# The second batch's keys turned by VectorE instead of TensorE, and entries of two hand-written orders moved, in an attention, feed-forward and routed-experts kernel

## The chip, the cores and the metric

One NeuronCore of a Trainium2 chip runs the whole kernel in one launch. The metric is device microseconds of one execution; several are made, and the median counts. TensorE multiplies and transposes into PSUM, VectorE (DVE), ScalarE (ACT) and GpSimd (POOL) do the element work, and SyncE (SP) issues most DMAs.

## The reference

```python
# attention: 4 batches, 8 heads of 64; 512 local and 32 global positions
k_all, v_all = concat([k_g, k_l]), concat([v_g, v_l])
out_g = softmax(scale * q_g @ k_all.T) @ v_all          # global queries see all keys
s_ll  = where(|i - j| <= 32, scale * q_l @ k_l.T, -1e9)  # local queries: a window ...
s_lg  = scale * q_l @ k_g.T                              # ... and the globals
out_l = softmax(concat([s_lg, s_ll])) @ concat([v_g, v_l])
x = concat([out_g, out_l]) as 2176 tokens x 512
# feed-forward with squared relu
x = (maximum(x @ w_in, 0) ** 2) @ w_out                  # 512 -> 2048 -> 512
# routed experts
do_compute = x @ w_skip > 0
e = argmax(x @ w_gate);  p = softmax(x @ w_gate)[e]      # 8 experts, each 512 -> 1024 -> 512
out = x;  out[do_compute] += p * (maximum(x @ w1[e], 0) @ w2[e])
```

## The kernel before, in words

The local tokens are cut into 8 blocks `j` of 256 (two tiles of 128 tokens, `a` and `b`), two blocks to a batch. Block `j` needs attention (`attention_block(j)`), then the feed-forward (`ffn_block(j)`), then routing (`route`, once for each tile), which fills a table of slots for the experts. The experts come last.

All engines run their instructions in the order in which the program emits them, and this order is written out by hand. `SEQ` is the list for blocks 0 to 2 and the feed-forwards of blocks 0 and 1; afterwards `EVEN` and `ODD` alternate: while `ffn_block(j)` runs, they emit attention of block `j+1` and the routing of block `j-1`. One pass of the loop with even `j` uses `EVEN`: that is `j` = 2, 4, 6. A word of a list emits one step:

- `F0`, `E0`, `I0`, `H0` (and 1; in `EVEN` and `ODD` plain `F`, `E`): one unit of a feed-forward. Units alternate between a first product (`first`, lines 803 to 805, 12 matmuls, then relu on ACT, line 807) and a second product (`second`, lines 828 to 830, 6 matmuls) that is emitted behind the squaring of the newer hidden block and its split into a high part `gh` (ACT, line 203) and a low part `gl` (line 204). The letter says which engine squares (`F`, `I`: VectorE, line 844; `E`, `H`: ScalarE, line 846) and which makes `gl` (`F`, `E`: GpSimd; `H`, `I`: VectorE).
- `Lk10`, `Lk11`: load the keys of batch 1, heads 0 to 3 and 4 to 7 (`load_k`). `2G`, `20` to `23`: in block 2, which opens batch 1, turn the global keys and the four head pairs of local keys into `kT` (`prep_globals`, `prep_k`). `2q` turns the queries.
- `2a`, `2b`: the next of six steps of a tile's attention. Step 1 emits the scores `sc` of all eight heads (line 484) with mask, maximum and exponentials of half of them (lines 497 to 505); step 2 the other half's; steps 3 and 4 transpose the weights (`ptr`, line 511); step 5 is the product with the values (`po`); step 6 transposes the result.
- `1g`, and `g` in `EVEN`: the next of eight steps of the global queries' attention: scores; transposes `gptr` and their copies `gpT`, `gpTg` (lines 615, 619); value products `gpo` (line 626) with their four scalings into `xg` (line 634); an empty step; and the same four again for the other heads.
- `R00`, `R01` (tiles of block 0), and `r`, `s` in `EVEN`: the next of five steps of `route`: 1 transposes the tile (`x2tr`, line 300) and makes a bf16 copy on ACT (line 713); 2 makes the other two bf16 thirds on VectorE (lines 703 to 705); 3 multiplies with the gates (`pl`, line 725) and finds the expert (VectorE); 4 counts (`pr`, lines 750 and 751) and works out the slot on VectorE (lines 752 to 776; line 766 is the last to read `pr`); 5 puts it in the table (`pt`, line 779).
- `C`, `D`: convert one weight tile (ACT line 271, the low part of the one before on GpSimd or VectorE, line 275). `V`: load value windows. `W`, `A`: fetch and reassemble weights.

PSUM has eight banks, by name of the tile's tag: two `tr` (all transposes, and half of each score tile), one `s`, one `o`, two `h`, two `x2`. In `EVEN`'s passes the tiles `po`, `gpo`, `pl`, `pr` and `pt` all have the tag `o`:

```python
BANKS = {"tr": 2, "s": 1, "o": 1, "h": 2, "x2": 2}
po = ps.tile([P, D], F32, tag=O_TAG, bufs=BANKS[O_TAG], name=f"gpo{b}_{g}")   # O_TAG "o"
pr = ps.tile([P, 2, E], F32, tag=O_TAG, bufs=BANKS[O_TAG], name=f"pr{t}")     # O_TAG "o" for j >= 2
```

Batches 2 and 3 already have their keys turned by VectorE; batches 0 and 1 by TensorE, four transposes of 128x128 for each pair of heads into a `tr` bank (line 376), copied to `kT` by two instructions (lines 378 and 383; on ACT in batch 1). The two ways want the keys loaded in different layouts: for TensorE 4 DMAs of 128 KB for four heads, in pieces of 64 numbers (256 bytes); for VectorE's 32x32 blocks 8 DMAs of 64 KB, in pieces of 32 numbers (128 bytes).

Of the kernel before, what the change touches and what calls it, by code (L numbers as in the profile page):

```python
# [22 lines left out]
    0b A V 0a W 0b V A 1q W W A 0b V 1a W W F0 A W E0 1a W W A W V 1a A F0 W 1a I0 A 1b L9 1a H0 V A A W V E0 W 1a  # L23
    X0 H0 A A E0 H0 W H0 A H0 W 1b E0 Lg1 A A W W A E0 1b W H0 A 1b E0 A H0 A E0 Lv00 A W W W 1g A I0 C 1b A 1g I0 W
    A D H0 Lv01 1g W E0 A E0 A I0 1g W C C 1g C W E0 A 1g Lq2 C Lk10 A H0 1g I0 2q A C C F0 2G Lk11 E0 I0 20 C 1b E0 21
    22 F0 F1 23 C D F0 H1 C C V R00 2a F1 D H1 E1 2a E1 D R00 2a H1 R00 R01 C H1 C C F1 I1 R01 V 2b R01 E1 D A F1
    2a E1 D C H1 2b F1 R00 2a I1 C C H1 D F1 V H1 R00 V F1 R01 C Lq3 E1 D E1 C C R01 F1 2b D C 2b H1 C C 1g F1 H1 2b
    2a E1 F1 D E1 F1 H1 Lv10 V 2b I1 V
"""

EVEN = """
    q E F F r E r a F a E lg F s F r E s E F g a s E a E a F g F r V a F g E r V E lv1 F b g s E F b E E b E V g b F
    b F b F g F s lk1 F g E V g lq F lk0 E
"""

# [17 lines left out]
TURNED = 3  # L53
# [6 lines left out]
def attention_ffn_routed_experts(  # L60
# [22 lines left out]
    nc = tc.nc  # L83
    B, H, SL, D = q_l.shape
# [5 lines left out]
    E, _, F = w1.shape  # L90
# [4 lines left out]
    TPB = SL // P  # L95
# [28 lines left out]
    def stage(name):  # L124
        return wpool.tile([P, 1024], F32, tag="w", name=f"st_{name}{arm[0]}")
# [3 lines left out]
    def pair(name):  # L129
        return ps.tile([P, 4, P], F32, tag="tr", bufs=2, name=name + arm[0])  # L130
# [160 lines left out]
    kT, kin, qT, qin, qgT, vgr = {}, {}, {}, {}, {}, {}  # L291
# [10 lines left out]
    def quadrants(o, src):  # L302
        for r in range(2):
            for half in range(2):
                c = SEG * (2 * r + half)
                for a in range(o.shape[1]):
                    nc.sync.dma_start(o[c:c + SEG, a], src(r)[:, a, :, SEG * half:SEG * (half + 1)])

    def load_k(b, z):
        if b == 0:  # L310
            kin[b, z] = stage(f"k{b}_{z}").rearrange("p (j h d) -> p j h d", h=4, j=TPB)
            t = stage(f"k{b}_{z}_in").rearrange("p (h j d) -> p h j d", h=4, j=TPB)
            nc.sync.dma_start(t, k_l[b, 4 * z:4 * z + 4].rearrange("h (p j) d -> p h j d", j=TPB))
            puts[f"{b}{z}"] = lambda: nc.scalar.copy(kin[b, z], t.rearrange("p h j d -> p j h d"))
            return
        if b < (TURNED + 1) // 2:
            kin[b, z] = stage(f"k{b}_{z}").rearrange("p (j h d) -> p j h d", h=4, j=TPB)
            for h in range(4):
                nc.sync.dma_start(kin[b, z][:, :, h, :], k_l[b, 4 * z + h].rearrange("(p j) d -> p j d", j=TPB))
            return  # L320
        kin[b, z] = stage(f"k{b}_{z}").rearrange("p (a n d) -> p a n d", a=2, d=SEG)
        pairs = k_l[b, 4 * z:4 * z + 4].rearrange("(a r) (n p) d -> r p a n d", r=2, p=SEG)
        quadrants(kin[b, z], lambda r: pairs[r])
# [39 lines left out]
        nc.scalar.copy(qgT[b], tr[:, :, 0:SG])  # L363

    def prep_k(b, p):
        if b >= (TURNED + 1) // 2:
            full = WIN * (KEYS // P)
            src = kin[b, p // 2][:, p % 2].rearrange("p n d -> p (n d)")
            threes = kT[b][:, p, 0:KEYS - SEG].rearrange("p (g c) -> p g c", c=P)[:, :, 0:WIN]
            nc.vector.transpose(out=threes, in_=src[:, 0:full].rearrange("p (g c) -> p g c", c=WIN))  # L370
            nc.vector.transpose(out=kT[b][:, p, KEYS - SEG:KEYS], in_=src[:, full:SL])
            return
        tr = pair(f"ktr{b}_{p}")
        for j in range(TPB):
            two = kin[b, p // 2][:, j, 2 * (p % 2):2 * (p % 2) + 2, :]
            nc.tensor.transpose(tr[:, j, :], two.rearrange("p r d -> p (r d)"), ident)
        q = WIN * (KEYS // P) // TPB
        nc.scalar.copy(
            kT[b][:, p, 0:KEYS - SEG].rearrange("p (g q j) -> p j g q", j=TPB, q=P // TPB)[:, :, :, 0:WIN // TPB],
            tr[:, :, 0:q].rearrange("p j (g q) -> p j g q", q=WIN // TPB),  # L380
        )
        put = nc.vector.tensor_copy if b == 0 else nc.scalar.copy
        put(kT[b][:, p, KEYS - SEG:KEYS].rearrange("p (q j) -> p j q", j=TPB), tr[:, :, q:P])
# [256 lines left out]
    def attention_block(j, S_TAG="s", O_TAG="o", G_TAGS=("s", "o")):  # L640

        b, z = divmod(j, TPB // 2)
        gens = {
            "a": attention(2 * j, S_TAG, O_TAG), "b": attention(2 * j + 1, S_TAG, O_TAG),
            "g": attention_global(b, *G_TAGS),
        }

        def emit(what):
            if what in gens:
                next(gens[what])  # L650
            elif what == "G":
                prep_globals(b)
            elif what == "q":
                prep_q(j)
            elif what in "0123":
                prep_k(b, int(what))
            elif what == "lq":
                if j + 1 < NB:
                    load_q(j + 1)
            elif what in ("lv0", "lv1"):  # L660
                load_v_global(b, int(what[2]))
            elif b + 1 < B:
                load_globals(b + 1) if what == "lg" else load_k(b + 1, int(what[2]))

        return emit
# [649 lines left out]
    with tc.manual_schedule():  # L1315
# [3 lines left out]
        def do(what):  # L1319
# [12 lines left out]
            elif what == "V":  # L1332
                load_v(*divmod(viewed[0], 2))
                viewed[0] += 1
            elif what[0] == "P":
                puts[what[1:]]()
            elif what == "L9":
                nc.sync.dma_start(w9[:, :, 0:E], w_gate.rearrange("(k p) e -> p k e", p=P))
                nc.sync.dma_start(w9[:, :, E:E + 1], w_skip.rearrange("(k p o) -> p k o", p=P, o=1))
            elif what[0] == "L":  # L1340
                load = {"g": load_globals, "k": load_k, "q": load_q, "v": load_v_global}[what[1]]
                load(*map(int, what[2:]))
            elif what[0] in "FEIH":
                square_on[0] = nc.vector if what[0] in "FI" else nc.scalar
                rest_on[0] = nc.gpsimd if what[0] in "FE" else nc.vector
                j = int(what[1])
                if j not in streams:
                    streams[j] = ffn_block(j, 1, (("x2", "x2"), ("s", "o"))[j])
                next(streams[j])
            elif what[0] == "R":  # L1350
                j, z = int(what[1]), int(what[2])
                if (j, z) not in routes:
                    routes[j, z] = route(*outs[j][z], *(("x2",) if j == 0 else ()))
                next(routes[j, z])
            else:
                j = int(what[0])
                if j not in emits:
                    emits[j] = attention_block(
                        j, *(("x2", "x2") if j == 2 else ("s", "o")), (("tr", "tr") if j == 1 else ("s", "o"))
                    )  # L1360
                emits[j](what[1:])
# [75 lines left out]
        for what in TAIL.split():  # L1437
            if what == "T":
                next(ffn, None)
            elif what in "XY":  # L1440
                j = "XY".index(what)
# [39 lines left out]
            elif what[0] in "gp":  # L1481
                e, j = map(int, what[1:])
# [226 lines left out]
```

## Time and profile before

| | |
|---|---|
| median of 3 runs | 692.17 us (690.86 to 692.66) |
| the profiled execution's own time | 692.0 us |
| its span, first to last instruction | 690.3 us |
| TensorE matmul busy | 663.4 us (96%) |
| TensorE weight load busy | 553.0 us (80%) |
| VectorE busy | 423.2 us (61%) |
| ScalarE busy | 344.4 us (50%) |
| GpSimd busy | 180.7 us (26%) |
| mean granted TensorE clock | 0.983 of full speed |

The profile is of one execution. Times in its rows are microseconds from the start of the span. A bracket behind a row is the time that the engine was idle before it, and the instruction that ended the wait.

### The profile page before, as it was taken

Reading aid. Unit: us, or ns where it says so; the run is one execution under the profiler, and the core shown is the slowest. Engines: PE = TensorE matmul, PEld = TensorE weight load, DVE = VectorE, ACT = ScalarE, POOL = GpSimd, SP = SyncE. Lnnn points to the kernel's source line nnn. Section 1 sums busy time; section 2 is a strip of 40 time slices with the busy share of each in tenths; the row PEclk is TensorE's granted clock in tenths of the full one; section 3 lists DMA queues with packets and bytes.
Section 4 is the critical chain, followed back from the end, with each engine's and each line's share of the span. In section 5 each row is a group of like instructions: output and inputs, shape, how many; then the busy total and the mean of one; then the engine's idle time right before and its main releaser. Section 6 shows DMA issues by size and latency. Waiting matters only on the chain. (4 is left out here: it accounts for less than half of the span.)

```text
span 690.3 us, 16621 instructions
## 1 busy us (share of the span) xinstructions
PE 663.4 (96%) x6545; PEld 553.0 (80%) x6545; DVE 423.2 (61%) x1142; ACT 344.4 (50%) x834; POOL 180.7 (26%) x236
## 2 busy tenths in 40 slices
PE   6689999999999999999999999999999999999996
PEld 4466668788888888888888888888987887898875
DVE  1899983874566377367456647535248535816984
ACT  5767567765534444453445453434344324615862
POOL 8000043354222212312222322222212242301321
PEclk8699999999999999999999999999999999999999
DMA  9999844047053441307243402210056588953920
GB/s 274 248 294 249 282 99 109 1 109 149 5 120 65 95 109 36 85 2 149 72 76 90 108 6 85 82 63 32 1 153 192 200 286 300 385 204 111 371 94 21
DMA packets 137503, 93.39 MB, mean 135 GB/s; under 512 B 103541, under 2 KB 110709, under 8 KB 137412
## 3 DMA queue, kind: packets, MB, share of 16 engines
q1 hardware_dynamic: 127104, 70.62, 38.2%
q10 hardware_dynamic: 8292, 15.48, 6.8%
q0 software_dynamic: 2016, 6.09, 2.5%
q8 instruction: 55, 0.90, 0.6%
q14 instruction: 36, 0.29, 0.1%
HBM read 79.91 MB, written 12.66 MB: 134 GB/s over the span
## 5 line engine op out<-in xcount | busy, mean ns | idle before, releaser
L204 POOL TENSOR_TENSOR gl<-g,gh 128x256 fp32r<-128x256 f32 x107 | 79.8, 746 | 238.7 <-ACT gh L203 94.5
L803 PE MATMUL h<-xh,w_in 128*128 128x256 f32 x464 | 134.1, 289 | 0.0
L805 PE MATMUL h<-xh,w_in 128*128 128x256 f32 x464 | 129.8, 280 | 0.2 <-POOL w_in L275 0.2
L804 PE MATMUL h<-xl,w_in 128*128 128x256 f32 x464 | 129.6, 279 | 0.0
L828 PE MATMUL acc<-w_out,gh 128*128 128x512 f32 x232 | 97.0, 418 | 1.2 <-ACT gh L203 1.2
L830 PE MATMUL acc<-w_out,gl 128*128 128x512 f32 x232 | 91.9, 396 | 0.2
L829 PE MATMUL acc<-w_out,gh 128*128 128x512 f32 x232 | 91.5, 395 | 0.0
L803 PEld LDWEIGHTS h<-xh,w_in 128*128 128x128 f32 x464 | 87.1, 188 | 4.5 <-issue 1.0
L804 PEld LDWEIGHTS h<-xl,w_in 128*128 128x128 f32 x464 | 87.2, 188 | 2.7 <-DVE xl L204 0.2
L805 PEld LDWEIGHTS h<-xh,w_in 128*128 128x128 f32 x464 | 87.1, 188 | 0.4 <-POOL w_in L275 0.4
L807 ACT ACTIVATE g<-h 128x256 f32<-128x256 f32 x128 | 48.7, 380 | 66.8 <-PE h L805 45.1
L203 ACT CAST gh<-g 128x256 fp32r<-128x256 f32 x116 | 47.1, 406 | 37.7 <-DVE g L844 35.6
L844 DVE TENSOR_TENSOR g<-h,g 128x256 f32<-128x256 f32 x53 | 22.1, 417 | 69.5 <-ACT g L807 69.4
L505 ACT ACTIVATE sm<-sm,mx 128x128 f32<-128x128 f32 x120 | 41.2, 391 | 43.1 <-DVE mx L502 43.1
L830 PEld LDWEIGHTS acc<-w_out,gl 128*128 128x128 f32 x232 | 43.5, 188 | 12.0 <-POOL gl L204 1.5
L828 PEld LDWEIGHTS acc<-w_out,gh 128*128 128x128 f32 x232 | 43.6, 188 | 8.4 <-ACT gh L203 1.7
L829 PEld LDWEIGHTS acc<-w_out,gh 128*128 128x128 f32 x232 | 43.7, 189 | 5.8
L275 POOL TENSOR_TENSOR w_in<-st_raw_in,w_in 128x512 fp32r<-128x512 f32 x10 | 13.2, 1326 | 74.7 <-ACT w_in L271 74.7
L497 DVE TENSOR_TENSOR sm<-sc,masks_slots 128x512 f32<-128x512 f32 x30 | 20.6, 687 | 14.7 <-PE sc L484 13.5
L846 ACT ACTIVATE g<-g 128x256 f32<-128x256 f32 x63 | 26.2, 415 | 4.1 <-ACT g L807 2.1
L826 PE MATMUL acc<-st_raw_out,gh 128*128 128x512 f32 x48 | 23.9, 618 | 0.8 <-ACT gh L846 0.8
L511 PE MATMUL ptr<-ident,sm 128*128 128x128 f32 x120 | 20.5, 290 | 2.5 <-ACT sm L505 2.4
(649 smaller groups left out, 1446.3 us busy)
## 6 DMA issues: line engine op xcount, KB each, us to landing
st_e<-in_moe_w_dram SPq DMA_DIRECT2D x46, 512.0 KB
st_raw_in<-in_moe_w_in_dram SPq DMA_DIRECT2D x16, 512.0 KB
st_raw_out<-in_moe_w_out_dram SPq DMA_DIRECT2D x16, 512.0 KB
st_e<-in_moe_w_dram ACTq DMA_DIRECT2D x12, 512.0 KB
x2d<-x ACTq DMA_DIRECT2D x19, 256.5 KB
vr<-in_v_l_dram SPq DMA_DIRECT2D x32, 128.0 KB
st_gv<-in_v_l_dram SPq DMA_DIRECT2D x8, 512.0 KB
out_dram<-x ACTq DMA_DIRECT2D x16, 256.0 KB
```

The source lines that it names most:

```text
L203: nc.scalar.copy(hi, src)
L204: (lo_engine or nc.vector).tensor_tensor(out=lo, in0=src, in1=hi.bitcast(F32), op=ALU.subtract)
L505: nc.scalar.activation(sm[:, hh, :], sm[:, hh, :], AF.Exp, bias=mx[:, hh:hh + 1], scale=SCALE, **sums)
L803: nc.tensor.matmul(h, lhsT=wh, rhs=xh[:, k, :], start=(k == 0), stop=False)
L804: nc.tensor.matmul(h, lhsT=wh, rhs=xl[:, k, :], start=False, stop=False)
L805: nc.tensor.matmul(h, lhsT=wl, rhs=xh[:, k, :], start=False, stop=(k == KD - 1))
L807: nc.scalar.activation(g, h, AF.Relu)
L826: nc.tensor.matmul(acc[z], lhsT=gh[:, c], rhs=w, start=first_one, stop=last_one)
L828: nc.tensor.matmul(acc[z], lhsT=gh[:, c], rhs=wh, start=first_one, stop=False)
L829: nc.tensor.matmul(acc[z], lhsT=gh[:, c], rhs=wl, start=False, stop=False)
L830: nc.tensor.matmul(acc[z], lhsT=gl[:, c], rhs=wh, start=False, stop=last_one)
L846: nc.scalar.activation(square, g, AF.Square)
```

## The change

Batch 1's keys are loaded and turned as those of batches 2 and 3: `load_k` and `prep_k` lose their middle way. In `SEQ` pair 22 is turned three feed-forward units later and pair 23 two; step 1 of `2a` (scores) comes one unit later, step 1 of `2b` one routing step and one unit later, step 2 of `2b` one unit later. In `EVEN` the third `g`, the first half's value products `gpo`, moves from behind the next `F` to ahead of the fourth step of `r`, so that `pr` follows it at once.

```diff
-    22 F0 F1 23 C D F0 H1 C C V R00 2a F1 D H1 E1 2a E1 D R00 2a H1 R00 R01 C H1 C C F1 I1 R01 V 2b R01 E1 D A F1
-    2a E1 D C H1 2b F1 R00 2a I1 C C H1 D F1 V H1 R00 V F1 R01 C Lq3 E1 D E1 C C R01 F1 2b D C 2b H1 C C 1g F1 H1 2b
+    F0 F1 C D F0 22 H1 C C 23 V R00 F1 2a D H1 E1 2a E1 D R00 2a H1 R00 R01 C H1 C C F1 I1 R01 V R01 E1 2b D A F1
+    2a E1 D C H1 F1 2b R00 2a I1 C C H1 D F1 V H1 R00 V F1 R01 C Lq3 E1 D E1 C C R01 F1 2b D C 2b H1 C C 1g F1 H1 2b
 EVEN = """
-    q E F F r E r a F a E lg F s F r E s E F g a s E a E a F g F r V a F g E r V E lv1 F b g s E F b E E b E V g b F
+    q E F F r E r a F a E lg F s F r E s E F g a s E a E a F g F g r V a F E r V E lv1 F b g s E F b E E b E V g b F
 def load_k(b, z):
-        if b < (TURNED + 1) // 2:
-            kin[b, z] = stage(f"k{b}_{z}").rearrange("p (j h d) -> p j h d", h=4, j=TPB)
-            for h in range(4):
-                nc.sync.dma_start(kin[b, z][:, :, h, :], k_l[b, 4 * z + h].rearrange("(p j) d -> p j d", j=TPB))
-            return
 def prep_k(b, p):
-        if b >= (TURNED + 1) // 2:
+        if b:
```

## Rows read from the trace of the kernel before

**Rows 1.** Windows: length, busy time of five engines, granted clock, DMA share, GB/s.
```profile
105.00:115.00 10.00, 9.46 (x68) 8.52 (x67) 2.14 (x5) 7.70 (x17) 2.13 (x3) 1.00 0.72 161
115.00:131.00 16.00, 15.18 (x166) 12.92 (x164) 11.83 (x32) 12.94 (x40) 6.47 (x6) 1.00 0.02 5
131.00:145.00 14.00, 13.21 (x206) 10.94 (x205) 12.64 (x39) 8.93 (x33) 7.07 (x8) 1.00 0.07 16
...
204.00:311.00 107.00, 107.00 (x1260) 93.29 (x1259) 61.51 (x198) 49.31 (x138) 25.89 (x33) 1.00 0.31 68
```

**Rows 2.** Timeline of TensorE where batch 1's keys are turned (start, length).
```profile
105.39 0.60 PE L376 MATMUL ktr<-ident,st_k 128*128 128x128 f32 x4
105.83 0.64 PE L463 MATMUL xtr<-ident,xt 128*128 128x128 f32 x4
...
107.73 0.60 PE L376 MATMUL ktr<-ident,st_k 128*128 128x128 f32 x4
108.87 0.66 PE L376 MATMUL ktr<-ident,st_k 128*128 128x128 f32 x4 [0.54 <-DVE xl L204]
```

**Rows 3.** Lines 370 and 371, VectorE's turning of later batches: shortest/median/longest ns.
```profile
L370 DVE STREAM_TRANSPOSE kT<-st_k x8: 635/667/670, 233.2 to 359.1; 128x480 f32<-128x480 f32 x8
L371 DVE STREAM_TRANSPOSE kT<-st_k x8: 168/168/169, 233.8 to 359.7; 128x32 f32<-128x32 f32 x8
```

**Rows 4.** Timeline of SP: issue of batch 1's keys, and of half of batch 2's.
```profile
97.87 7.25 SPq L319 DMA_DIRECT2D st_k<-in_k_l_dram  x8
...
206.27 5.17 SPq L307 DMA_DIRECT2D st_k<-in_k_l_dram  x8
```

**Rows 5.** A window behind batch 2's load, columns as in the first group.
```profile
213.00:215.00 2.00, 2.00 (x13) 1.49 (x11) 0.69 (x1) 1.94 (x7) 0.29 (x1) 1.00 0.01 1
```

**Rows 6.** Timeline of TensorE around the moved steps of block 2.
```profile
120.95 0.50 PE L828 MATMUL acc<-w_out,gh 128*128 128x512 f32 x1 [0.74 <-ACT gh L203]
...
126.06 0.46 PE L725 MATMUL pl<-w,x2T 128*128 128x27 bf16 x12
...
131.18 1.16 PE L484 MATMUL sc<-kT,qT 64*32 64x128 f32 x64
...
132.66 0.41 PE L725 MATMUL pl<-w,x2T 128*128 128x27 bf16 x10 [0.18 <-DVE x2T L705]
```

**Rows 7.** Timeline of VectorE: a square, and the last operands of the two gate products.
```profile
118.83 0.41 DVE L844 TENSOR_TENSOR g<-h,g 128x256 f32<-128x256 f32 x1
...
124.98 0.20 DVE L705 TENSOR_TENSOR w<-w,w 128x36 bf16<-128x36 f32 x1
...
131.91 0.69 DVE L705 TENSOR_TENSOR x2T<-x2tr,x2T 128x512 bf16<-128x512 f32 x1
```

**Rows 8.** Waits of TensorE's weight loads, 200 to 560 us: total, times, longest.
```profile
PEld gpo L626 <- DVE sizes L766: 2.3, 3, 0.8
```

**Rows 9.** Timeline of TensorE around the value products, first pass of `EVEN`.
```profile
198.46 0.18 PE L750 MATMUL pr<-oh,tri 128*128 128x8 bf16 x1
...
199.77 0.40 PE L830 MATMUL acc<-w_out,gl 128*128 128x512 f32 x1
200.53 0.65 PE L626 MATMUL gpo<-st_gv,gpT 128*32 128x64 f32 x32 [0.35 <-DVE sizes L766]
...
201.35 0.38 PE L803 MATMUL h<-xh,w_in 128*128 128x256 f32 x1
...
202.75 0.28 PE L805 MATMUL h<-xh,w_in 128*128 128x256 f32 x1
203.12 0.33 PE L779 MATMUL pt<-ohs,ohl 128*128 128x136 f32 x1
```

**Rows 10.** Timeline of VectorE, the same place.
```profile
198.04 0.67 DVE L615 COPY gpT<-gptr 128x512 f32<-128x512 f32 x1
...
201.20 0.34 DVE L776 TENSOR_SCALAR ohl<-iota_s,rt 128x128 fp32r<-128x128 f32 x1
...
201.91 1.16 DVE L634 TENSOR_SCALAR xg<-gpo,grs 32x64 f32<-32x64 f32 x4
```

## Prediction

> **What bounds the kernel now.** I first read the busy time by stretch. TensorE is the bound where it matters: from 204 to 311 us it is busy 107.00 of 107 us, at a granted clock of 1.00 (the level of 2.4 GHz), and nothing there could absorb a delay [rows 1]. In the stretch of batch 1's keys and block 2 it is idle 0.54, 0.82 and 0.79 us of 10, 16 and 14, 2.15 in all [rows 1]. So I count every edit in TensorE's time: instructions that leave its queue, and waits that go or come. The clock is at its upper level in all these stretches before, and no edit opens a long hole, so I price no change of it. After that I read the timeline of TensorE at each edited place, and then VectorE's at the same time, because VectorE ends most of the waits. Last I looked at what holds the waits that repeat: of the weight loads' waits from 200 to 560 us, the largest that comes once in every pass of `EVEN` is the value products' for line 766, the last reader of `pr`, 2.3 us in 3 times [rows 8]. `gpo` and `pr` share the one bank `o`.
>
> **The keys.** Out of TensorE's queue go 16 transposes. A group of four holds it from 105.39 to 105.83, 0.44 us [rows 2]; four groups are 1.76. The third group also waited for a `tr` bank that block 1's `xl` still read: from 107.73 to 108.87 are 1.14, of which 0.44 are the group before it, so 0.70 goes as well [rows 2]. Together 2.46.
>
> VectorE gets four pairs of turnings, 0.67 and 0.17 us each, 3.4 us [rows 3]. It is busy 2.14 of the 10 us from 105 to 115 [rows 1], so I cost them at nothing; without that cover the feed-forward's `gl`, which VectorE makes for the `I` and `H` units, would be late by what they exceed it. ScalarE loses eight copies, where it is busy 7.70 of 10 [rows 1]: this pulls relus and casts forward, but TensorE's waits there are counted already.
>
> SP issues 16 DMAs instead of 8. Batch 2's eight took 5.17 to issue from 206.27 [rows 4], and from 213 on nothing moves [rows 5]: landed within 6.7 us. Batch 1's first eight start at 97.87 [rows 4], so they land by 104.6, ahead of 105.39 where pair 20 was turned [rows 2]. The second eight follow at 103.0 at the latest and land by 109.8. Pair 22 was turned at 108.87 [rows 2] and now stands three units later, less the 2.46 gained: 110.6. (A unit takes about 1.4 us: a `first` issues from 201.35 to 202.75, a `second` from behind `pr` at 198.5 to 199.77 [rows 9].) Margin about one microsecond, cost nothing; below I price its failure. The value loads queue behind them on SP and start some 2 us later; they are read by block 2's value products, which come behind both gate products, after 132 [rows 6].
>
> The Trainium skill, page "DMA: Bandwidth & Descriptors", sections "Specifications" and "Why small descriptors are slow (HBM only)", speaks against this edit: pieces below 512 bytes don't reach line rate, and each packet costs about 3 cycles beside its 32-byte beats. By it 128-byte pieces take 14 cycles where one of 256 takes 11, an estimate of 1.27 times the wire time for the same bytes. The rows of batch 2 were measured with 128-byte pieces, so the sum already holds it.
>
> **The moved steps of block 2.** With `2a`'s scores behind the `F1` unit, `gh` of that unit is no longer cast behind four exponentials, and the wait of 0.74 at 120.95 goes [rows 6]. With `2b`'s scores behind the `E1` unit a like wait further on may go: of the 0.79 idle from 131 to 145 [rows 1] 0.18 is another [rows 6], so at most 0.6.
>
> Two waits come. First, block 0's gate product `pl` at 126.06 has its last operand at 125.18, a slack of 0.88 [rows 6, 7]. TensorE now gets there 2.46 + 0.74 = 3.2 sooner. VectorE's chain to that operand starts with the scores; these come 2.46 sooner but one unit (1.4) later, about 1.05, and the unit's square (0.41 [rows 7]) leaves the chain: 1.45 sooner. New wait: 3.2 - 1.45 - 0.88 = 0.9. Second, the other tile's `pl` stood behind the scores, which began at 131.18; its operand ended at 132.60 [rows 6, 7]. Now it stands where the scores stood, and would wait 1.4 instead of 0.18: 1.2 lost, as TensorE and VectorE have by then come forward about equally. A third, small: `F1`'s `second` now follows block 0's transpose at once, and its `gh` is just being cast; I take 0.2. Behind a waiting `pl` the whole queue of TensorE stands. Sum of the moves: 0.74 + 0.6 - 0.9 - 1.2 - 0.2 = -1.0, a loss.
>
> So `SEQ` gives 2.46 - 1.0, about 1.4 us. Bounds: all idle time goes and nothing comes, 1.76 + 2.15 = 3.9; or the new waits take all, 0.
>
> **`EVEN`, three passes.** Before, TensorE waits in front of `gpo` and in front of `pt`. At `gpo` the wait is between 0.35 (the matmul's own bracket [rows 9]) and 0.77 (the weight load's, 2.3 over 3 [rows 8]); I take 0.55, nearer the matmul, which is what holds the queue. At `pt` the last matmul, begun at 202.75, ends at 203.03 and `pt` starts at 203.12 [rows 9]; with the spacing of the overlapped matmuls the wait is 0.1 to 0.35, I take 0.25. Sum 0.8 for a pass, which the edit can remove.
>
> After, `gpo` stands where `pr` stood, 198.46 [rows 9]. Its operand `gpT` is copied by 198.71 [rows 10]; with a handover of 0.05 (`pt` started 0.05 after line 634 ended at 203.07 [rows 9, 10]) it waits 0.3. It holds TensorE 0.82 (200.53 to 201.35 [rows 9]), to about 199.6. Then comes `pr`, which needs the bank: it must wait until VectorE has scaled all of `gpo`, four instructions in 1.16 [rows 10], with a handover on each side. So it starts at 200.9, 1.3 after TensorE was free. Before, a whole unit of 1.4 us lay between `gpo` and the next user of the bank, and hid just this. New waits 1.6, old 0.8: 0.8 lost in a pass. `pt` should not wait: VectorE's slot arithmetic runs from the copy's end, 198.71, to 201.54 [rows 10], at most 2.8; from 200.9 that is 203.7, and TensorE, with two units of 1.4 and 1.5 behind `pr`, gets to `pt` at 203.9. Behind `pr` stand the feed-forward units, so the wait is in the open. Three passes: 2.4. Bounds: with the old waits at their upper ends (1.1) 1.5; at their lower (0.45) 3.5.
>
> **Sum.** 692.0 (the profiled execution; its span of 690.3 and 1.7 around it) - 1.4 + 2.4 = 693.0. The median of the runs is 0.17 above that execution, so 693.2. A difference under 0.3% (2.1 us) can't be told from none here.
>
> **Rivals.**
> Forecast, about the same: the two parts nearly cancel, 690.1 (keys and moves near their ceiling) to 694.2 (`EVEN` at its upper bound). Chance 0.57.
>
> Slower, the moves eat the keys' gain: the waits at the two `pl` grow because VectorE's chain through the thirds comes forward less than I think. For it: two waits on VectorE come and it is busy 12.64 of 14 us there [rows 1]. Against: ScalarE's relief. With no gain left it is 692.2 + 2.4 = 694.6; it decides as soon as `SEQ` gives less than 0.3. Chance 0.19.
>
> Slower, the keys land late: pair 22 waits on VectorE, and behind it the `gl` of the next unit and so TensorE. It begins to cost once the second load lands later than 110.6, and each microsecond then costs one; from one microsecond on (111.6) it decides, 694.3 to 697. For it: the margin is one microsecond, and the value loads share the queues (a DMA share of 0.72 there [rows 1]). Against: they come behind on SP. The Trainium skill's packet rule, told above, points this way; no row here shows 256-byte pieces alone. Chance 0.07.
>
> Faster, `pr` doesn't wait for the scalings: then only the 0.3 is new, a pass gains 0.5, and with `SEQ` it is 692.2 - 1.5 - 1.4 = 689.3. Against: the same bank made `gpo` wait for `pr`'s readers in all three passes [rows 8]. Or `SEQ` reaches its ceiling of 3.9 with `EVEN` at its lower bound of 1.5: 689.8. Together 0.17.
>
> **How the numbers follow.** The predicted time is the forecast's 693.2. Faster by over 0.3% is the last rival, 0.17; slower the two before it, 0.26; the rest 0.57. The range runs from 689.3, the price of the first faster case, to 695.2, above the price of the first slower rival and in the middle of the late keys': some 0.1 lies outside on each side.
>
> **What would show it.** Right: `ktr` of batch 1 gone; at the two `pl` of block 0 brackets from VectorE's line for the thirds, together over 1 us; the wait at 120.95 gone; in each pass of `EVEN` a bracket of more than a microsecond in front of `pr`, released by VectorE's `xg`, and none in front of `pt`. Wrong: `pr` right behind `gpo` without a wait; a wait of VectorE's turnings on the keys' DMA; or the moved steps of block 2 without any wait, with block 2 ending over 3 us sooner.

## The result: 696.55 us, slower, and the profile after

The changed kernel took 696.55 us (median of 6 runs, 695.88 to 697.25), the kernel before 692.17 beside it: ratio 1.0064, 95% interval 1.0051 to 1.0077, a loss of 4.4 us. The forecast of 693.2 is 3.35 us too low, and the time lies above the range's end of 695.2. The profiled execution took 696.84 us with a span of 695.1; before 692.0 and 690.3. Lines of the changed kernel have numbers lower by 5 than before's from line 321 on.

First the busy time by stretch after, with the columns of [rows 1]:

```profile
105.00:115.00 10.00, 9.90 (x65) 8.71 (x64) 5.67 (x15) 6.72 (x15) 3.99 (x5) 1.00 0.72 145
115.00:131.00 16.00, 13.77 (x155) 11.32 (x153) 12.22 (x32) 10.75 (x36) 6.29 (x6) 1.00 0.08 18
131.00:145.00 14.00, 13.41 (x203) 11.08 (x204) 9.04 (x33) 7.46 (x27) 5.49 (x7) 1.00 0.09 20
204.00:311.00 107.00, 107.00 (x1203) 93.53 (x1202) 60.26 (x193) 48.95 (x138) 25.92 (x33) 0.99 0.31 69
```

From 105 to 115 TensorE idles 0.10 us where it idled 0.54 [rows 1]: the wait for the `tr` bank is gone. From 115 to 131 it idles 2.23 where it idled 0.82. The last row has a clock of 0.99 where it had 1.00; that hundredth is opened up below.

TensorE's waits in block 2, to set beside [rows 6], and SP's issue of the keys, beside [rows 4]:

```profile
98.69 8.30 SPq L307 DMA_DIRECT2D st_k<-in_k_l_dram  x16
...
121.71 0.50 PE L823 MATMUL acc<-w_out,gh 128*128 128x512 f32 x1 [0.25 <-ACT gh L203]
124.10 0.45 PE L720 MATMUL pl<-w,x2T 128*128 128x27 bf16 x12 [0.38 <-DVE w L700]
130.53 0.19 PE L720 MATMUL pl<-w,x2T 128*128 128x27 bf16 x1 [1.23 <-DVE x2T L699]
131.26 0.41 PE L720 MATMUL pl<-w,x2T 128*128 128x27 bf16 x10 [0.54 <-DVE x2T L700]
133.10 1.16 PE L479 MATMUL sc<-kT,qT 64*32 64x128 f32 x64
139.37 0.50 PE L823 MATMUL acc<-w_out,gh 128*128 128x512 f32 x1 [0.24 <-ACT gh L203]
147.56 0.50 PE L823 MATMUL acc<-w_out,gh 128*128 128x512 f32 x1 [0.66 <-ACT gh L203]
```

The wait of 0.74 at 120.95 [rows 6] is gone. In its place stand the second gate product's two waits, 1.77 together, 0.38 at the first gate product, and two that the prediction does not have: 0.25 at 121.71 and 0.66 at 147.56.

The wait at 139.37 is shorter than its like before:

```profile
136.89 0.50 PE L828 MATMUL acc<-w_out,gh 128*128 128x512 f32 x1 [0.48 <-ACT gh L203]
```

Then the first and the second pass of `EVEN`, beside [rows 9]:

```profile
197.02 0.63 PE L608 MATMUL gptr<-ident,pg 128*128 128x128 f32 x4
...
199.32 0.65 PE L621 MATMUL gpo<-st_gv,gpT 128*32 128x64 f32 x32
...
201.48 0.17 PE L745 MATMUL pr<-oh,tri 128*128 128x8 bf16 x1 [1.27 <-DVE xg L629]
...
203.48 0.63 PE L825 MATMUL acc<-w_out,gl 128*128 128x512 f32 x1
203.91 0.41 PE L798 MATMUL h<-xh,w_in 128*128 128x256 f32 x1
...
205.97 0.23 PE L774 MATMUL pt<-ohs,ohl 128*128 128x136 f32 x1
...
314.33 0.64 PE L608 MATMUL gptr<-ident,pg 128*128 128x128 f32 x4
...
318.82 0.17 PE L745 MATMUL pr<-oh,tri 128*128 128x8 bf16 x1 [1.27 <-DVE xg L629]
...
320.12 0.40 PE L825 MATMUL acc<-w_out,gl 128*128 128x512 f32 x1
...
321.77 0.23 PE L774 MATMUL pt<-ohs,ohl 128*128 128x136 f32 x1
```

The bracket ahead of `pr` is the one forecast. But the same product of 512 columns takes 0.63 us behind it in the first pass and 0.40 in the second. The windows say why (columns as before, the granted clock is third from the end):

```profile
200.00:201.00 1.00, 0.22 (x8) 0.15 (x9) 0.70 (x3) 0.00 (x0) 0.63 (x1) 1.00 0.83 267
201.00:202.00 1.00, 0.52 (x4) 0.47 (x4) 0.89 (x7) 0.00 (x0) 0.00 (x0) 0.96 1.19 333
202.00:203.00 1.00, 1.00 (x4) 0.77 (x3) 0.86 (x8) 0.00 (x0) 0.00 (x0) 0.50 1.35 198
...
204.00:205.00 1.00, 1.00 (x7) 1.00 (x6) 0.00 (x0) 0.40 (x1) 0.52 (x1) 0.50 0.35 75
205.00:206.00 1.00, 1.00 (x9) 1.00 (x9) 0.00 (x0) 0.00 (x0) 0.21 (x1) 0.83 0.13 21
```

TensorE's clock stands at 0.50, the level of 1.2 GHz, from about 202 to 205, right behind the idle time ahead of `pr`.

Who waited for whom, 196 to 445 us, beside [rows 8]; and VectorE in the first pass, beside [rows 10]:

```profile
PE pr L745 <- DVE xg L629: 3.8, 3, 1.3
...
PEld gpo L621 <- DVE gpT L610: 1.0, 3, 0.4
```

```profile
198.59 0.67 DVE L610 COPY gpT<-gptr 128x512 f32<-128x512 f32 x1
...
200.27 1.16 DVE L629 TENSOR_SCALAR xg<-gpo,grs 32x64 f32<-32x64 f32 x4 [0.82 <-PE gpo L621]
...
203.29 0.34 DVE L771 TENSOR_SCALAR ohl<-iota_s,rt 128x128 fp32r<-128x128 f32 x1
```

`pr` starts 0.05 after the scalings end at 201.43. The weight load of `gpo` waits for the copy of its operand, 0.4 us at the longest, where 0.3 was forecast.

**Two yardsticks.** Runs of one kernel spread over some 2 us, and block 2 starts up to 1.3 us earlier or later from one execution to the next, so I compare two lengths inside each trace. The first, "block 2", runs from the `qtr` product that waits near 100 us to the first `gptr` of `EVEN`; the second is a pass, from `gptr` to `pt`. Before, they run between these rows and [rows 9]:

```profile
99.86 0.66 PE L400 MATMUL qtr<-ident,st_q 128*128 128x128 f32 x4 [0.74 <-DVE xg L634]
...
196.46 0.64 PE L613 MATMUL gptr<-ident,pg 128*128 128x128 f32 x4
```

All kernels by these yardsticks, taken from such rows (us; ratios against the kernel before, measured beside each):

| kernel | ratio (95%) | block 2 | pass 1 | pass 2 | pass 3 |
|---|---|---|---|---|---|
| before | 1 | 96.60 | 6.66 | 6.66 | 6.66 |
| after | 1.0064 (1.0051-1.0077) | 96.94 | 8.95 | 7.44 | 7.42 |
| swap of `EVEN` alone | 1.0041 (1.0028-1.0054) | 96.60 | 8.97 | 7.44 | 7.42 |
| keys and moves, no swap | 1.0015 (1.0006-1.0024) | 96.94 | 6.66 | 6.66 | 6.67 |
| keys alone | 0.9975 (0.9964-0.9985) | 94.49 | 6.66 | 6.67 | 6.68 |
| moves alone | 1.0062 (1.0049-1.0074) | 100.04 | 6.67 | 6.67 | 6.67 |
| keys, move 1 | 0.9971 (0.9960-0.9981) | 94.93 | 6.66 | 6.66 | 6.67 |
| keys, move 2 | 0.9980 (0.9971-0.9989) | 95.59 | 6.67 | 6.66 | 6.67 |
| keys, move 3 | 0.9978 (0.9969-0.9988) | 95.25 | 6.65 | 6.67 | 6.66 |
| after, `gpo` in bank `s` | 1.0013 (1.0003-1.0023) | 98.48 | 6.63 | 6.68 | 6.66 |
| before, `gpo` in bank `s` | 0.9964 (0.9951-0.9978) | 96.55 | 5.99 | 5.98 | 6.00 |
| keys, `gpo` in bank `s` | 0.9932 (0.9918-0.9945) | 94.52 | 5.99 | 5.98 | 6.00 |
| swap, filled (transposes) | 1.0103 (1.0086-1.0120) | 96.57 | 7.41 | 7.43 | 7.43 |
| swap, filled (wide) | 1.0104 (1.0086-1.0122) | 96.60 | 7.42 | 7.44 | 7.42 |
| swap in pass 1 | 1.0036 (1.0022-1.0050) | 96.59 | 7.41 | 6.68 | 6.67 |
| swap in passes 2, 3 | 1.0028 (1.0018-1.0038) | 96.56 | 6.66 | 7.44 | 7.43 |

### The profile page after: what moved, and what is told of

The parts are those of the page before. It is cut to its first block, busy times and chain, and to the rows that moved or that the text cites. A ratio compares the mean times of both kernels' runs of the same rounds, so it can differ in the third digit from the quotient of the medians.

```text
span 695.1 us, 16612 instructions
## 1 busy us (share of the span) xinstructions
PE 664.4 (96%) x6529; PEld 553.9 (80%) x6529; DVE 422.1 (61%) x1150; ACT 340.3 (49%) x826; POOL 179.2 (26%) x236
```

## Experiments

### The change taken apart

**The swap alone** (the kernel before with the new `EVEN`):

```diff
-g F r V a F g E r V E
+g F g r V a F E r V E
```

> Only the order of EVEN is changed: gpo ahead of pr, all else as before. Theory A (each pass pays the wait of pr for the scalings, 0.8 us net, and the pass in which the clock's rows fell from 1.00 to 0.50 right behind that wait pays 1.5 us more): +3.8 us against the kernel before, with a clock of 0.50 for about 3 us behind pr in at least one pass. Rival B (the clock fell by chance of that profiled execution; only the waits are real): +2.4 us, all three passes at +0.8 and the clock at 1.00.

Passes of 8.97, 7.44 and 7.42, the clock again at 0.50 behind the first `pr` alone: in the trace +3.85, as theory A had it. The timed runs gave +2.8 us (1.9 to 3.7), between the two theories.

**Keys and moves without the swap** (the changed kernel with the old `EVEN`):

> The changed kernel with EVEN in its old order: keys turned by VectorE and the moved steps of block 2 remain. Theory A (the first part's gain is eaten by three waits in block 2, at 124 to 131 us and at 147.6 us): 0 to +0.7 us against the kernel before. The prediction's sum: -1.4 us. Rival B (the swap costs only its waits, so the rest of the loss lies here): +2 us.

Block 2 is 0.34 longer than before, the passes are before's; timed +1.0 us (0.4 to 1.7). The prediction's gain of 1.4 is not there.

**The keys alone** (the changed kernel with the old `EVEN`, and in `SEQ` the steps of 2a and 2b where they were; 22 and 23 at their later places):

```diff
-V R00 F1 2a D H1
+V R00 2a F1 D H1
...
-V R01 E1 2b D A F1
+V 2b R01 E1 D A F1
...
-C H1 F1 2b R00 2a I1
+C H1 2b F1 R00 2a I1
```

> Keys of batch 1 turned by VectorE, the last two pairs at their later places, the score steps of block 2 and EVEN as before. Theory A (16 transposes at 1.76 us and the 0.70 us wait for the tr bank leave TensorE's queue, the moved score steps are what gives the gain back): -2.0 to -2.5 us. Rival (the stretch up to 150 us is paced by VectorE and ScalarE, so whatever TensorE saves returns as waits further on, moves or no moves): between -0.7 us and +0.3 us, with more idle time of TensorE from 115 to 150 us than the 2.2 us of the kernel before.

Block 2 is 2.11 shorter than before, and the gain stays: timed -1.7 us (-1.0 to -2.5). TensorE's timeline here:

```profile
114.01 0.45 PE L479 MATMUL sc<-kT,qT 64*32 64x128 f32 x16 [0.28 <-DVE kT L365]
118.21 0.50 PE L823 MATMUL acc<-w_out,gh 128*128 128x512 f32 x1 [0.74 <-ACT gh L203]
129.92 0.41 PE L720 MATMUL pl<-w,x2T 128*128 128x27 bf16 x10 [0.18 <-DVE x2T L700]
134.15 0.50 PE L823 MATMUL acc<-w_out,gh 128*128 128x512 f32 x1 [0.47 <-ACT gh L203]
```

The waits of before are all still there, each about 2.7 sooner by the span's clock; 0.65 of that is block 2's earlier start in this execution, 99.21 for 99.86. One is new, 0.28 of the scores on VectorE's last turning. The rival, a gain that comes back as waits, falls.

**The moves alone** (the kernel before, with only the three steps of 2a and 2b moved):

> Only the score steps of block 2 are moved one step later; keys turned by TensorE at their old places, EVEN as before. Theory A (the moves lose by themselves: longer waits at the two gate products and at the unit behind the second score step): +1 to +2.5 us; the prediction's terms, without the keys' head start, which made 0.9 of the loss: about 0. Rival (the moves are neutral and the keys' gain is lost by itself): -0.3 to +0.3 us.

Block 2 is 3.44 longer, timed +4.3 us (3.4 to 5.1). The moves lose by themselves, more than either theory had it; with the keys they lose 96.94 - 94.49 = 2.45. Most of the 0.99 between the two is a wait that stands here alone,

```profile
115.95 0.50 PE L828 MATMUL acc<-w_out,gh 128*128 128x512 f32 x1 [0.58 <-ACT gh L203]
```

and the 0.28 of the scores on VectorE's last turning, which the moves take away where VectorE turns the keys.

### The three moves one by one, with the keys

Each is the kernel with the keys alone, and one line of the diff above undone.

> The run with the keys alone (0.9975 of the kernel before), and only the first of the three moved steps: 2a's scores behind the F1 unit. Theory A (the wait of 0.74 us ahead of that unit goes, waits of 0.25 and 0.4 us come at the next unit and at the first gate product): 0 to -0.3 us against the keys alone; from the qtr wait to the third gptr 94.3 us in place of 94.49. The prediction's terms (+0.74 -0.9 -0.2): +0.4 us.

> The run with the keys alone, and only the second moved step: 2b's scores behind the E1 unit, so that the second gate product stands ahead of them. Theory A (that gate product waits twice for VectorE's thirds, 1.8 us in all, where the scores covered it): +1.3 to +1.7 us against the keys alone. The prediction's terms (-0.6 +1.2): +0.6 us.

> The run with the keys alone, and only the third moved step: 2b's second softmax half, which has no work for TensorE, behind the F1 unit. Theory A (its four exponentials stand ahead of the next unit's relu and casts on ScalarE, and the wait of 0.66 us at 147.6 us with its weight load comes from there): +0.6 to +1.0 us against the keys alone, with a wait of TensorE for gh near 145 us. The prediction gave this step no price: 0. Rival (that wait belongs to the second move): 0.

The run times can't part these three from the keys alone; block 2 does: +0.44, +1.10 and +0.76, together 2.30 of the 2.45. TensorE at the second gate product, first with the first move alone, then with the second, and the second's later wait:

```profile
131.12 0.41 PE L720 MATMUL pl<-w,x2T 128*128 128x27 bf16 x10 [0.54 <-DVE x2T L700]
```

```profile
129.98 0.19 PE L720 MATMUL pl<-w,x2T 128*128 128x27 bf16 x1 [0.66 <-DVE x2T L699]
130.70 0.41 PE L720 MATMUL pl<-w,x2T 128*128 128x27 bf16 x10 [0.54 <-DVE x2T L700]
...
138.81 0.50 PE L823 MATMUL acc<-w_out,gh 128*128 128x512 f32 x1 [0.24 <-ACT gh L203]
```

For the first move theory A was wrong, and the prediction's sum (0.4) came out, but not by its terms: the first gate product waits 0.37 instead of 0.9, and TensorE is 0.1 ahead of the keys alone until the second gate product, whose wait grows from 0.18 to 0.54. The second lies between the prediction's 0.6 and theory A's 1.3. For the third theory A was right. TensorE in the kernel with the third move:

```profile
135.40 0.50 PE L823 MATMUL acc<-w_out,gh 128*128 128x512 f32 x1 [0.47 <-ACT gh L203]
146.25 0.50 PE L823 MATMUL acc<-w_out,gh 128*128 128x512 f32 x1 [0.46 <-ACT gh L203]
```

The wait at 146.25 comes with this move alone. In the changed kernel ScalarE shows what stands ahead of that unit's `gh`:

```profile
143.73 0.40 ACT L500 ACTIVATE sm<-sm,mx 128x128 f32<-128x128 f32 x1 [2.14 <-DVE mx L497]
...
145.29 0.36 ACT L802 ACTIVATE g<-h 128x256 f32<-128x256 f32 x1
...
147.10 0.41 ACT L203 CAST gh<-g 128x256 fp32r<-128x256 f32 x1
```

ScalarE idles 2.14 us until VectorE has the maxima of the second half of 2b, then runs its four exponentials, and only then the unit's relu, two casts of weight tiles (1.2 us, there without the move too), the unit's square and its cast. TensorE had been done with that unit's first products since 144.1.

### The bank, and the order

**`gpo` in its own bank, new order and old.** The edit is the same in both kernels:

```diff
-emit = attention_block(j + 1) if j + 1 < NB else None
+emit = attention_block(j + 1, G_TAGS=("s", "s")) if j + 1 < NB else None
```

> The changed kernel, but in the passes of EVEN gpo takes the bank s instead of o, so that pr needn't wait until VectorE has scaled gpo. Theory A (the shared bank is what holds pr, and the hole it leaves is what the fall of the clock follows): no wait ahead of pr, clock 1.00 behind it, a pass from gptr to pt in 6.1 to 6.4 us instead of 8.95, 7.44 and 7.42; about 691.5 us, the kernel before less 0.4. Rival (pr waits for oh and its own chain on VectorE when it stands behind gpo, whatever the bank): the wait stays within 0.3 us of 1.27.

> The kernel before, with gpo in the bank s in the passes of EVEN; no other edit. Theory A (the waits ahead of gpo and of pt come from the bank shared with pr and pt): a pass from gptr to pt in 5.9 to 6.1 us instead of 6.66, three passes -1.6 to -2.3 us. Rival (pt waits for VectorE's slot arithmetic anyway, and the wait only moves there): 6.4 us or more a pass, -0.8 us at best.

In the new order `pr` follows `gpo` at once, as theory A said, but a pass takes 6.66, not 6.1 to 6.4. TensorE there:

```profile
201.64 0.31 PE L621 MATMUL gpo<-vgr,gpTg 32*32 32x64 f32 x8
201.89 0.18 PE L745 MATMUL pr<-oh,tri 128*128 128x8 bf16 x1
...
205.40 0.33 PE L774 MATMUL pt<-ohs,ohl 128*128 128x136 f32 x1 [0.38 <-DVE ohl L771]
```

VectorE in the same stretch:

```profile
202.01 1.16 DVE L629 TENSOR_SCALAR xg<-gpo,grs 32x64 f32<-32x64 f32 x4 [0.82 <-PE gpo L621]
203.19 0.15 DVE L747 TENSOR_SCALAR rt<-rt 128x1 f32<-128x1 f32 x1
...
205.01 0.34 DVE L771 TENSOR_SCALAR ohl<-iota_s,rt 128x128 fp32r<-128x128 f32 x1
```

Now `pt` waits: VectorE scales `gpo` from 202.01 on and only then turns to the slot arithmetic, whose last step ends at 205.35. Theory A had not counted that. In the old order a pass takes 5.99, 0.67 less than before, and the kernel gains 2.5 us (1.5 to 3.4). So the shared bank made `pr` wait, and the old order is 0.67 a pass better than the new one once the bank is out of the way.

**Keys alone, with `gpo` in its own bank:**

> Keys turned by VectorE (as in the run with the keys alone, 0.9975 of the kernel before), and gpo in the bank s, all score steps and EVEN in the old order. If the two gains are independent: the keys' -2.0 and the own bank's -1.6 to -2.3, about 688 us. If both draw on the same slack of VectorE: no better than the keys alone, 690 us.

687.39 us (687.09 to 687.70) beside 692.07: the gains add within their intervals, and this kernel takes 0.7% less than the kernel before, the shortest time of all.

### The clock

**The hole filled.** In the kernel with the swap alone, behind `gpo` in the three passes:

```diff
+            if b and not g:
+                fill = pair(f"fill{b}")
+                for z in range(10):
+                    nc.tensor.transpose(fill[:, z % 4, :], ident, ident)
```

The second filled kernel has five products of 512 columns of `w_out`'s tiles there instead.

> The kernel before with the order of EVEN changed, as in the run of the swap alone (1.0041 of the kernel before), and behind gpo ten transposes of the identity, 1.1 us by the spacing of the keys' transposes, whose result nothing reads: TensorE works through most of the time in which pr waits. Theory A (the clock falls because TensorE stands idle ahead of pr): clock 1.00 behind pr in all passes, pass 1 from gptr to pt in 7.4 to 7.6 us like the other two; -0.7 to -1.5 us against the swap alone. Rival (the clock falls in this place for another reason): rows of 0.50 behind pr again, and no gain.

> The swap of EVEN alone, and behind gpo five products of 512 columns (1.2 us by the acc rows) in place of the ten transposes, 15 instructions instead of 30; their result is not read. Theory A (the clock falls behind the hole, and the loss of the first filled kernel lay in the hole of 2.84 us with no releaser at the experts' code and in the fall behind it): 7.4 to 7.5 us from gptr to pt in every pass, clock 1.00 there, and without such a hole 694.2 us, 0.5 to 1 us below the swap alone. Rival (filling itself costs time, as the first filled kernel had it): 697 us or more without any such hole.

In both, all three passes take 7.41 to 7.44 and the clock stays at 1.00 there. Both kernels are nevertheless 4.3 us slower than the swap alone by ratio. What the profiles show stands elsewhere, at the experts; first TensorE in the first filled kernel, then its windows:

```profile
605.52 0.31 PE L1060 MATMUL ewh_a<-xp,e1l 128*128 128x320 f32 x1 [2.84 <-issue]
```

```profile
605.00:606.00 1.00, 0.48 (x4) 0.47 (x4) 0.00 (x0) 0.07 (x1) 0.00 (x0) 1.00 1.05 385
606.00:607.00 1.00, 1.00 (x6) 1.00 (x6) 0.49 (x1) 0.37 (x1) 0.00 (x0) 0.50 1.06 377
```

A hole of 2.84 us with no releaser, and a fall of the clock behind it. The second filled kernel has one of 2.41 at 588.5, with a fall behind it too. So theory A's forecast of the total failed, by a hole at another place in each of the two profiled executions; that the other executions, as slow, had one too is not shown. Its forecast for the passes came true. That filling keeps the clock up isn't shown by it: six passes without a fall could be chance, since behind most unfilled holes of this kind the clock doesn't fall either (next experiment).

**The swap in some passes only** (the kernel before; `SWAPPED` is the new `EVEN`; the second kernel has `j > 2`):

```diff
-for what in (ODD if j % 2 else EVEN).split():
+for what in (ODD if j % 2 else SWAPPED if j == 2 else EVEN).split():
```

> The kernel before with the order of EVEN changed in its first pass alone (EVEN runs three times; the other two keep the old order). Theory A (that pass pays 0.8 us of waits and, because the clock falls there whenever the hole stands in it, 1.5 us more): +2.3 us against the kernel before, a fall to 0.50 behind pr near 201 us. Rival (the fall is a matter of the single execution): the waits alone in most executions, +0.8 us in the median, and the profiled one may show either.

> The kernel before with the order of EVEN changed in its second and third pass alone. Theory A (the fall belongs to the first pass's place): waits of 0.77 us twice, +1.5 us, clock 1.00 behind both pr. Rival (the clock falls behind the first hole of this kind, wherever it stands): a fall to 0.50 behind pr near 314 us, 1.5 us more, +3 us.

Neither profiled execution shows a fall, though all three holes of 1.27 us are there: pass 1 takes 7.41, like the others. So neither the first pass's place nor being the first hole brings the fall by itself; it differs from execution to execution. That the place makes it likelier is not excluded: of all the holes ahead of `pr` in unfilled kernels, 2 of 3 in pass 1 were followed by a fall and none of 6 in the other two. The times point the same way: with the swap in pass 1 alone they lost 2.5 us (1.5 to 3.5), where the trace's pass lost 0.75; in passes 2 and 3 1.9 (1.2 to 2.6), where the trace's passes lost 1.55. The profiled execution of the first kernel took 692.71 us, its four others 694.34 to 695.78. That these had the fall would fit, but no trace shows it, and their mean granted clock (0.987 and 0.988 beside 0.991) doesn't decide it: that of the kernel before ran from 0.980 to 0.990 with no bearing on the time.

## Why the prediction was wrong, step by step

- **Keys, 2.46: nearly right.** The run with the keys alone gained 2.11 in block 2. Most of the missing 0.35 is the 0.28 for which the scores wait on VectorE's last turning; VectorE's turnings, costed at nothing, were off by that. The keys landed in time: no turning waits for a DMA. The Trainium skill's packet rule ("DMA: Bandwidth & Descriptors", section "Why small descriptors are slow (HBM only)") was weighed in the prediction; no wait here shows its price. Another rule of the Trainium skill, "VectorE: DVE Perf Modes", section "Rules for kernel authors", gives a 128x128 transpose to TensorE where the result may lie in PSUM. This case neither bears it out nor speaks against it, since VectorE turns blocks of 32x32 here, which the other layout of the loads made possible; with TensorE the bound and VectorE partly idle, that gained 2.11 us.
- **Moved steps, -1.0: the first step that failed.** They cost 2.45. Of the three edits I priced two: the third, 2b's second softmax half behind the `F1` unit, stands in the diff and in no term of the sum. It has no work for TensorE, but VectorE's maxima and four exponentials that now run ahead of a unit's casts: 0.76. Of the two that were priced, the second cost 1.10 for 0.6. Its gate product came near the forecast: with this move alone it waits 0.66 + 0.54 = 1.20, for 1.4 (with the first move also made, 1.77). The gain of 0.6 was mis-sized, since I had put its upper bound into the sum: the like wait further on only shrank, from 0.48 to 0.24. The first came to 0.44 for 0.36, by luck: its waits stand elsewhere than forecast. `SEQ`, forecast at +1.4 with a floor of 0, thus lost 0.34 in the trace. That is the outcome of the rival "the moves eat the keys' gain", but not its reason: the waits at the two `pl`, 0.38 + 1.77 = 2.15, did not grow beyond the forecast's 0.9 + 1.4.
- **`EVEN`, 0.8 a pass: right in the waits.** Passes 2 and 3 cost 0.78 and 0.76 more than before. `pr` waits 1.27 (forecast 1.3), `pt` doesn't.
- **"No edit opens a long hole, so I price no change of it" (the clock): the second step that failed.** My own sum had 1.3 us of idle TensorE in every pass. In the profiled execution the clock fell behind one of the three, and pass 1 cost 2.29 instead of 0.8.
- **The signs.** All that the prediction named for being right are there: no `ktr` of batch 1, 2.15 us of brackets at the two `pl`, no wait of 0.74, over a microsecond ahead of `pr` in each pass, none ahead of `pt`. They stood for the terms that were priced, and so could not show the two that weren't.
- **The sum repaired.** 693.0, + 1.45 for the moves, + 0.35 for the keys, is 694.8, still inside the range; + 1.5 for one fall of the clock it is 696.3, beside 696.84 of the profiled execution. The rest, 0.5, lies within what the stretch from the last `pt` of `EVEN` to the end varies by from one execution to another (256.95 us before, 257.55 after, 255.9 to 257.8 in the experiments without a hole at the experts).

What stays open: in how many of the timed executions of the changed kernel the clock falls, and so how much of the median's loss is its doing; and why some of these holes are followed by a fall and others, equally long, are not.

## What to carry to other kernels

Go through a reordering edit by edit: a step with no instruction on the bounding engine still moves the queues of the others, and 0.76 us of this loss came from such a step. When two products share a bank, moving them next to each other puts the reader of the first into the open; another bank for one of them was worth 2.5 us here, while the new order cost 0.77 a pass with the shared bank and 0.67 with its own. An upper bound is no estimate: the 0.6 taken whole gave 0.24. A wait that leaves the bounding engine idle can cost more than its length: behind 2 of 9 waits of 1.27 us the clock fell, for 1.5 us more, so price it as a chance beside the wait.

## What the hardware showed that I had not expected

**Falls of the clock behind short holes.** Between 50 and 680 us of the profiled executions of all these kernels TensorE's clock was below 1.00 in five places, each time right behind a hole: behind 2 of 9 waits of 1.27 or 1.28 us ahead of `pr` (both in pass 1), behind 1 of the 4 pairs of waits ahead of the second gate product (1.22 + 0.54, in the changed kernel with its own bank, which is why its block 2 is 1.54 longer), and behind the holes of 2.41 and 2.84 at the experts, but not behind one of 1.65 there. Each fall went to 0.50 and lasted about 3.4 us by the windows; the first pass with it took 1.5 us longer than the passes without. That the hole is what brings the fall is argued from this neighbourhood; no edit here showed it.

**Holes with no releaser at the experts.** 0.81 us with the swap alone, 1.65 in the profiled execution of the kernel before with its own bank (which took 692.73, its four others 689.10 to 690.04), 2.41 and 2.84 in the filled kernels, none in the kernel before. The DMA queues of the filled kernel show what may stand behind them (queue and kind, packets, MB, share):

```profile
q8 instruction: 56, 0.92, 0.6%
```

That is 16.4 KB a packet; before's page has 55, and so have those of the second filled kernel and of the swap alone, so the number doesn't part kernels with holes from those without. The Trainium skill, "Runtime: NRT & Kernel Launch", section "Instruction fetch mechanics", says that each engine fetches its instructions by DMA in blocks of 16 KiB, and that a taken branch out of the blocks at hand stalls it. The packets' size agrees; that these holes wait for such a block no run here shows.
